# Linear attention with a SwiGLU block: query norms in pieces and another order of copies in the opening of batch 0

## The chip, the cores and the metric

The kernel runs on one core of one Trainium2 chip. The metric is the device time of one execution in microseconds; a median is given where a kernel ran several times. TensorE (PE, with its weight loads PEld), VectorE (DVE), ScalarE (ACT) and GpSimd (POOL) each work through a queue of their own in program order; SyncE (SP) and POOL also issue DMAs.

## The reference

```python
# q, k, v: (8 batches, 8 heads, 576 positions, 64)
q_s = exp(q - max(q, axis=-1));  q_s /= sum(q_s, axis=-1)   # softmax over the 64 features
k_s = exp(k - max(k, axis=2));   k_s /= sum(k_s, axis=2)    # softmax over the positions
kv  = einsum('bhsd,bhse->bhde', k_s, v)                     # 64 x 64 for each head
x   = einsum('bhsd,bhde->bhse', q_s, kv)                    # -> 4608 tokens x 512
g, val = x @ w_gate, x @ w_val                              # 512 -> 1536
out = (g * sigmoid(g) * val) @ w_out                        # 1536 -> 512, float32
```

## The kernel before, in words

Heads are taken in two groups of four (G = 0 and 1). Each of the 128 partitions holds 9 consecutive positions of one head of a pair (T = 9), so a group's q is a tile of 128 x 2 x 576. `BANKS` splits the nine positions into pieces of 5 and 4, as one PSUM bank takes five transposed 128x128 blocks and four the other.

For a group of queries, `exp_of` makes the exponentials on ScalarE, `norm_sum` their sums over 64 features and the reciprocals on VectorE (`rs`, `rr`), and `norm_mul` scales them (`qs`, VectorE). `turn_pe` transposes the scaled queries on TensorE into PSUM (`tp`), and `turn_out` copies them to SBUF (`qt`). For keys, `exp_of` makes `ek`; in batch 0 `key_sum` sums it over positions with small matmuls into `ks`, and its reciprocal `kvr` is made on VectorE. `kv_first` makes K^T V in 36 small matmuls, and `scale_first` scales it by `kvr` into `kn`, half 0 on ScalarE, half 1 on the engine that is given. `x_mm` multiplies `qt` by `kn` into PSUM (`xp`), and `x_out` copies that into `xt`, the transposed input of the feed-forward block: head pair half 0 on ScalarE and half 1 on VectorE.

Everything stands in a `tc.manual_schedule()`: the order in the text is the order of each engine's queue. In the opening SP issues the loads of q and k of both groups; POOL issues v of both groups once k of group 0 has landed, and then the weights in slices of columns (`w_slice`, gate and value in turn, slices of 128, 128, 128, 256, 384, 512), and w_out last. `spin(n)` is n matmuls on zeros that keep TensorE busy; the second call starts with the first sums of group 0. Then comes batch 0 (this is what the diff touches), and behind it `m_unit(0, 576, m)` for the twelve blocks of 128 columns of d_ff: gate matmuls `g_ps` and value matmuls `u_ps`, then silu on ScalarE and the product on VectorE. The first of them takes the four 128-row parts of `xt` by pairs (`by_group`), group 0's pair first.

After it the kernel makes output blocks (`o_mm`), attention of batch b+1 and the feed-forward block of earlier tokens in turn, in chunks of 448 and 512 tokens. PSUM has eight banks, all from one pool (`psp`), so a tile takes the bank that was freed eight tiles before.

Of the kernel before, what the change touches and what calls it, by code (L numbers as in the profile page):

```python
# [8 lines left out]
FP32 = mybir.dt.float32  # L9
BF16 = mybir.dt.bfloat16  # L10
# [5 lines left out]
def kernel(  # L16
# [10 lines left out]
    nc = tc.nc  # L27
# [6 lines left out]
    T = S // 64  # L34
# [3 lines left out]
    BANKS = ((0, 5), (5, T))  # L38
# [3 lines left out]
    at = ctx.enter_context(tc.tile_pool(name="at", bufs=2))  # L42
# [4 lines left out]
    def bank(name):  # L47
        return psp.tile([128, 512], FP32, tag="ps", name=name)
# [57 lines left out]
    def copy(eng, out, in_):  # L106
        if eng is nc.scalar:
            nc.scalar.copy(out=out, in_=in_)
        else:
            eng.tensor_copy(out=out, in_=in_)  # L110
# [3 lines left out]
    st = {}  # L114

    def exp_of(what, b, G, pieces=((0, T),)):
        s = st.setdefault((b, G), {})
        e = s["e" + what] = at.tile([128, T, 2, 64], BF16, tag="e" + what, name="e" + what)
        src = raw[what, b, G].rearrange("p h (t d) -> p t h d", d=64)
        for t0, t1 in pieces:  # L120
            nc.scalar.activation(out=e[:, t0:t1], in_=src[:, t0:t1], func=AF.Exp)  # L121
# [7 lines left out]
    def norm_sum(b, G, pieces=((0, T),)):  # L129
        s = st[b, G]  # L130
        eq2 = s["eq"].rearrange("p t h d -> p (t h) d")
        rs = at.tile([128, 2 * T], FP32, tag="rs", name="rs")
        first = None
        for t0, t1 in pieces:
            i = nc.vector.reduce_sum(  # L135
                out=rs[:, 2 * t0:2 * t1], in_=eq2[:, 2 * t0:2 * t1, :], axis=mybir.AxisListType.X
            )
            first = first or i
        rr = s["rr"] = at.tile([128, 2 * T], FP32, tag="rr", name="rr")
        nc.vector.reciprocal(out=rr, in_=rs)  # L140
        return first

    def norm_mul(b, G, pieces=((0, T),), engs=None):
        s = st[b, G]
        eq2 = s["eq"].rearrange("p t h d -> p (t h) d")
        qs = s["qs"] = at.tile([128, T, 128], BF16, tag="qs", name="qs")
        for (t0, t1), eng in zip(pieces, engs or (nc.vector, nc.vector)):
            n = 2 * (t1 - t0)
            last = eng.tensor_mul(  # L149
                qs[:, t0:t1, :].rearrange("p t (h d) -> p (t h) d", d=64),  # L150
                eq2[:, 2 * t0:2 * t1, :],
                s["rr"][:, 2 * t0:2 * t1].to_broadcast([128, n, 64]),
            )
        return last

    def turn_pe(b, G, i):
        s = st[b, G]
        if i == 0:
            s["qt"] = at.tile([128, T, 128], BF16, tag="qt", name="qt")
        t0, t1 = BANKS[i]  # L160
        tp = s["tp", i] = psp.tile([128, 1024], BF16, tag="ps", name="tp")
        for t in range(t0, t1):
            j = t - t0
            nc.tensor.transpose(  # L164
                out=tp[:, j * 128:(j + 1) * 128], in_=s["qs"][:, t, :], identity=ident
            )

    def turn_out(b, G, i, eng):
        s = st[b, G]
        t0, t1 = BANKS[i]  # L170
        copy(
            eng,
            s["qt"][:, t0:t1, :],
            s["tp", i][:, 0:(t1 - t0) * 128].rearrange("p (t c) -> p t c", c=128),
        )
# [19 lines left out]
    def x_mm(b, G, i):  # L195
        s = st[b, G]
        t0, t1 = BANKS[i]
        xp = [bank("xp") for _ in range(2)]
        for g in range(2):
            for h in range(2):  # L200
                r = slice(64 * h, 64 * h + 64)
                nc.tensor.matmul(
                    out=xp[h][64 * g:64 * g + 64, 0:64 * (t1 - t0)],
                    lhsT=s["kn"][r, g, :],
                    rhs=s["qt"][r, t0:t1, 64 * g:64 * g + 64],
                    start=True, stop=True,
                )
        return xp

    def x_out(b, G, i, xp, engs=(nc.scalar, nc.vector)):  # L210
        t0, t1 = BANKS[i]
        n = 64 * (t1 - t0)
        c0 = b * S + 64 * t0
        for h in (h for h in range(2) if engs[h] is not None):
            copy(engs[h], xt[:, 2 * G + h, c0:c0 + n], xp[h][:, 0:n])
# [137 lines left out]
    with tc.manual_schedule():  # L353
# [16 lines left out]
        for vb in vbs:  # L370
            nc.vector.memset(vb[:, :, :, 64:65], 1.0)

        exp_of("q", 0, 0, BANKS)
        exp_of("k", 0, 0)
        exp_of("q", 0, 1, BANKS)
        first = norm_sum(0, 0, BANKS)
        norm_mul(0, 0, BANKS)
        norm_sum(0, 1, BANKS)

        for c0, n in ((0, 128), (128, 128), (256, 128), (384, 256), (640, 384), (1024, 512)):  # L380
            w_slice(wg, moe_w_gate, c0, n)
# [3 lines left out]
        def spin(n, after=None):  # L385
            idle = bank("idle")
            for _ in range(n):
                i = nc.tensor.matmul(out=idle, lhsT=zero[:, 0:128], rhs=zero, start=True, stop=True)  # L388
                if after is not None:
                    tc.add_manual_dep(i.ins, after.ins.name, SYNC, reason="start of the warm-up")  # L390
                    after = None

        def key_sum(G):
            s = st[0, G]
            ks = bank("ks")
            for t in range(T):
                nc.tensor.matmul(
                    out=ks[:, 0:2], lhsT=s["ek"][:, t, :, :].rearrange("p h d -> p (h d)"), rhs=sel,
                    start=(t == 0), stop=(t == T - 1),
                )  # L400
            s["kvr"] = at.tile([128, 2], FP32, tag="kvr", name="kvr")
            nc.vector.reciprocal(out=s["kvr"], in_=ks[:, 0:2])

        def kv_first(G, t0=0, t1=T):
            s = st[0, G]
            if t0 == 0:
                s["kv"] = [bank("kv") for _ in range(2)]
            for t in range(t0, t1):
                for g in range(2):
                    for h in range(2):  # L410
                        nc.tensor.matmul(
                            out=s["kv"][g][HALF[h], 0:64], lhsT=s["ek"][HALF[g], t, h, :],
                            rhs=v16[G][HALF[g], h, 64 * t:64 * t + 64],
                            start=(t == 0), stop=(t == T - 1),
                        )

        def scale_first(G, eng1):
            s = st[0, G]
            kn = s["kn"] = at.tile([128, 2, 64], BF16, tag="kn1", name="kn1")
            nc.scalar.mul(kn[:, 0, :], s["kv"][0][:, 0:64], s["kvr"][:, 0:1])  # L420
            if eng1 is nc.scalar:
                nc.scalar.mul(kn[:, 1, :], s["kv"][1][:, 0:64], s["kvr"][:, 1:2])
            else:
                nc.vector.tensor_scalar_mul(kn[:, 1, :], s["kv"][1][:, 0:64], s["kvr"][:, 1:2])

        spin(8)
        spin(6, first)
        key_sum(0)
        turn_pe(0, 0, 0)
        turn_pe(0, 0, 1)  # L430
        turn_out(0, 0, 0, nc.scalar)
        exp_of("k", 0, 1)
        turn_out(0, 0, 1, nc.scalar)
        norm_mul(0, 1, BANKS)
        spin(6)
        kv_first(0)
        key_sum(1)
        scale_first(0, nc.scalar)
        turn_pe(0, 1, 0)
        turn_pe(0, 1, 1)  # L440
        turn_out(0, 1, 0, nc.vector)
        turn_out(0, 1, 1, nc.vector)
        xp0 = x_mm(0, 0, 0), x_mm(0, 0, 1)
        kv_first(1, *BANKS[0])
        kv_first(1, *BANKS[1])
        x_out(0, 0, 0, xp0[0], (nc.scalar, None))
        scale_first(1, nc.vector)
        x_out(0, 0, 0, xp0[0], (None, nc.vector))
        x_out(0, 0, 1, xp0[1])
        xp1 = x_mm(0, 1, 0), x_mm(0, 1, 1)  # L450
        x_out(0, 1, 0, xp1[0])
# [18 lines left out]
        exp_of("q", 1, 0)  # L470
        exp_of("q", 1, 1)
        norm_sum(1, 0)
        norm_mul(1, 0)
        norm_sum(1, 1)
        p = [None, None]
# [11 lines left out]
        i = norm_mul(1, 1)  # L487
# [117 lines left out]
```

The softmax here doesn't subtract the row's maximum and nothing guards it: scores larger than these inputs give would overflow.

## Time and profile before

| | us |
|---|---|
| median of 5 runs | 311.88 (311.48 to 312.81) |
| the profiled execution | 311.86 |
| its span, first to last instruction | 310.0 |
| TensorE busy in the span | 301.4 (97%) |
| VectorE busy | 161.6 (52%) |
| ScalarE busy | 146.2 (47%) |
| first gate matmul of the feed-forward block | starts at 14.22 |

Times within the span count from its start. Busy time of TensorE is rough, as matmuls overlap and their ends are modelled; the start-to-start distance of matmuls says more. In the timeline's lines the numbers are start and length, then engine, line and operation, the tile written and the tiles read, shapes, the count, and in brackets the idle time before and who ended it.

### The profile page before, as it was taken

What the parts mean: (1) busy time and instruction counts of PE and PEld (TensorE: products, weight loads), DVE (VectorE), ACT (ScalarE), POOL (GpSimd) and SP (SyncE); (2) the same over time, 40 slices, a digit from 0 to 9 for tenths busy, and PEclk for the clock granted to TensorE, in tenths of its full rate; (3) what the DMA queues carried; (4) which work ended last, traced back from release to release, by engine and by line L of the source; (5) the groups of instructions that cost most, each with busy time, mean ns of one, the idle gap of its engine ahead of it and who ended that gap; (6) DMA issues with size and microseconds to landing.
All of it is one profiled execution on the core that took longest, in us unless ns stands there. A gap on an engine that the chain in (4) does not pass through costs nothing.

```text
span 310.0 us, 5442 instructions
## 1 busy us (share of the span) xinstructions
PE 301.4 (97%) x2157; PEld 149.8 (48%) x2182; DVE 161.6 (52%) x286; ACT 146.2 (47%) x214; POOL 32.1 (10%) x39
## 2 busy tenths in 40 slices
PE   6999999999999999999999999999999999999995
PEld 2578745555444444454444444444444444444443
DVE  3844477945854566365826492639353334433421
ACT  5743469785674375547464737455143113312300
POOL 2960011511100110002000200000000000000000
PEclk9999999999999999999999999999999999999999
DMA  7999999999346815490739352605310302020133
GB/s 275 183 194 207 273 388 389 348 247 378 73 83 196 332 28 118 121 375 33 144 72 354 102 118 61 188 0 107 71 36 0 70 10 58 3 68 8 26 71 103
DMA packets 43018, 45.78 MB, mean 148 GB/s; under 512 B 19568, under 2 KB 28272, under 8 KB 42992
## 3 DMA queue, kind: packets, MB, share of 16 engines
q1 hardware_dynamic: 34096, 39.95, 43.3%
q0 software_dynamic: 8752, 5.31, 12.0%
q8 instruction: 17, 0.28, 0.4%
q10 hardware_dynamic: 144, 0.16, 0.2%
q14 instruction: 9, 0.07, 0.1%
HBM read 37.75 MB, written 9.44 MB: 152 GB/s over the span
## 4 chain that ended last, share of the span: by engine, by line
PE 92%; DMA 4%; POOL 1%; issue 1%; ACT 0%; SPq 0%; DVE 0%
PE u_ps L284 30%; PE g_ps L284 30%; PE o_ps L317 29%; DMA wv<-in_moe_w_val_dram 2%; DMA k<-in_k_dram 2%; PE kv L189 2%; PE xp L245 1%; PE o_ps L338 1%; POOL wg L96 0%; POOL v L361 0%; PE tp L164 0%; POOL v L358 0%; POOL wv L96 0%; ACT xt L259 0%; SPq L77 0%
## 5 line engine op out<-in xcount | busy, mean ns | idle before, releaser
L291 ACT ACTIVATE sg<-g_ps 128x512 bf16<-128x512 f32 (+2 forms) x120 | 64.7, 554 | 133.9 <-PE g_ps L284 120.4
L293 DVE TENSOR_TENSOR hr<-sg,u_ps 128x512 bf16<-128x512 bf16 (+3 forms) x120 | 72.6, 617 | 86.8 <-PE u_ps L284 80.1
L284 PE MATMUL g_ps<-xt,wg 128*128 128x512 bf16 (+2 forms) x473 | 110.9, 358 | 0.5
L284 PE MATMUL u_ps<-xt,wv 128*128 128x512 bf16 (+2 forms) x479 | 111.1, 358 | 0.1
L317 PE MATMUL o_ps<-wo,hr 128*128 128x512 bf16 x403 | 92.5, 379 | 0.9 <-issue 0.2
L284 PEld LDWEIGHTS <-wv 128*128 128x128 bf16 x480 | 46.9, 98 | 46.7 <-DMA wv<-in_moe_w_val_dram 0.4
L284 PEld LDWEIGHTS <-wg 128*128 128x128 bf16 x480 | 46.2, 98 | 45.6 <-issue 0.6
L317 PEld LDWEIGHTS <-hr 128*128 128x128 bf16 x420 | 40.9, 98 | 48.6
L110 DVE COPY o_sb<-o_ps 128x512 f32<-128x512 f32 x33 | 22.4, 680 | 39.0 <-PE o_ps L317 35.4
L124 POOL CAST vb<-v 128x1152 bf16<-128x1152 f32 x14 | 17.1, 1227 | 136.9 <-DMA v<-in_v_dram 134.8
L135 DVE TENSOR_REDUCE rs<-eq 128x18 f32<-128x1152 bf16 (+2 forms) x18 | 21.7, 1214 | 13.1 <-ACT eq L121 13.1
L149 DVE TENSOR_TENSOR qs<-eq,rr 128x1152 bf16<-128x1152 bf16 (+2 forms) x18 | 21.7, 1216 | 0.1
L121 ACT ACTIVATE eq<-q 128x1152 bf16<-128x1152 f32 (+2 forms) x18 | 18.3, 1051 | 5.1 <-DMA q<-in_q_dram 5.0
L121 ACT ACTIVATE ek<-k 128x1152 bf16<-128x1152 f32 (+2 forms) x17 | 17.9, 1101 | 1.0 <-DMA k<-in_k_dram 1.0
L291 ACT ACT_TABLE_LOAD x12 | 15.4, 1283 | 0.2
L121 ACT ACT_TABLE_LOAD x11 | 14.1, 1283 | 0.2
L388 PE MATMUL idle<-zero 128*128 128x512 bf16 x20 | 7.8, 554 | 2.8 <-DVE rs L135 1.6
L259 ACT CAST xt<-xp 128x512 bf16<-128x512 f32 x14 | 7.8, 586 | 4.0 <-PE xp L245 4.0
L260 DVE CAST xt<-xp 128x512 bf16<-128x512 f32 x14 | 9.0, 683 | 0.7 <-PE xp L245 0.7
L189 PEld LDWEIGHTS <-ek 64*64 64x64 bf16 x504 | 6.3, 107 | 1.7 <-ACT ek L121 0.4
L189 PE MATMUL kv<-vb,ek 64*64 64x65 bf16 x504 | 6.7, 194 | 0.0
L245 PE MATMUL xp<-qt,kn 64*64 64x512 bf16 (+1 forms) x112 | 6.7, 292 | 0.0
(44 smaller groups left out, 66.6 us busy)
## 6 DMA issues: line engine op xcount, KB each, us to landing
q<-in_q_dram SPq DMA_DIRECT2D x16, 576.0 KB, 5.1
out_dram<-o_sb SPq DMA_DIRECT2D x70, 128.0 KB, 2.4
k<-in_k_dram SPq DMA_DIRECT2D x12, 576.0 KB, 7.4
v<-in_v_dram SPq DMA_DIRECT2D x12, 576.0 KB, 9.0
wo<-in_moe_w_out_dram POOLq DMA_DIRECT2D x4, 384.0 KB, 15.3
k<-in_k_dram SPq DMA_DIRECT2D x4, 320.0 KB, 8.2
k<-in_k_dram SPq DMA_DIRECT2D x4, 256.0 KB, 8.4
v<-in_v_dram SPq DMA_DIRECT2D x2, 320.0 KB, 7.1
```

The lines of the kernel that those rows point to most:

```text
L110: eng.tensor_copy(out=out, in_=in_)
L121: nc.scalar.activation(out=e[:, t0:t1], in_=src[:, t0:t1], func=AF.Exp)
L124: return nc.gpsimd.tensor_copy(out=vbs[G][:, :, :, 0:64], in_=raw["v", b, G].rearrange("p h (t d) -> p t h d", d=64),)
L135: i = nc.vector.reduce_sum(out=rs[:, 2 * t0:2 * t1], in_=eq2[:, 2 * t0:2 * t1, :], axis=mybir.AxisListType.X)
L149: last = eng.tensor_mul(qs[:, t0:t1, :].rearrange("p t (h d) -> p (t h) d", d=64), eq2[:, 2 * t0:2 * t1, :], s["rr"][:, 2 * t0:2 * t1].to_ ...
L189: nc.tensor.matmul(out=kv[g][HALF[h], c:c + 65], lhsT=ek[HALF[g], t, h, :], rhs=vbs[G][HALF[g], t, h, :], start=(t == 0), stop=(t == T - 1),)
L245: nc.tensor.matmul(out=o[h][HALF[g], c:c + 64 * (t1 - t0)], lhsT=kn[HALF[h], g, G, :], rhs=qt[G][HALF[h], t0:t1, 64 * g:64 * g + 64], star ...
L260: nc.vector.tensor_copy(out=xt[:, 2 * G + 1, c0:c0 + 512], in_=main[G][1])
L284: nc.tensor.matmul(out=gu[a][i][:, 0:w_], lhsT=(wg, wv)[a][:, kk, ms], rhs=xt[:, kk, c:c + w_], start=(kk == 0), stop=(kk == KT - 1),)
L291: nc.scalar.activation(out=sg[:, 0:w_], in_=g_ps[:, 0:w_], func=AF.Silu)
L293: nc.vector.tensor_mul(hr[:, m, r:r + w1], sg[:, 0:w1], u_ps[:, 0:w1])
L317: nc.tensor.matmul(out=o_ps, lhsT=hr[:, m, r0:r0 + 128], rhs=wo[:, m, :], start=(m == 0), stop=(m == MT - 1),)
```

## The change

Four things, all in batch 0's opening. First, `norm_sum` makes a reciprocal for each piece right after its sum, and is called piece by piece, as are `norm_mul` and (for q of group 1) `exp_of`; tiles are made at the first call. Second, the key sums' reciprocal leaves `key_sum` and becomes `key_recip`, placed on its own. Third, the order: the first transposes of group 0 and their copy stand ahead of the key sums and of the second exp piece of group 1; the copy of group 1's first transposes stands on VectorE ahead of the scaling of its second piece; those transposes stand ahead of K^T V of group 0. The copy of x of group 0 is one call for both engines, so that VectorE copies its half before it scales `kn` of group 1. Fourth, the second `spin` has 4 matmuls instead of 6. SP's and POOL's queues keep their order.

```diff
     def norm_sum(b, G, pieces=((0, T),)):
...
         for t0, t1 in pieces:
-            i = nc.vector.reduce_sum(
-                out=rs[:, 2 * t0:2 * t1], in_=eq2[:, 2 * t0:2 * t1, :], axis=mybir.AxisListType.X
-            )
+            r = slice(2 * t0, 2 * t1)
+            i = nc.vector.reduce_sum(out=s["rs"][:, r], in_=eq2[:, r, :], axis=mybir.AxisListType.X)
+            nc.vector.reciprocal(out=s["rr"][:, r], in_=s["rs"][:, r])
             first = first or i
-        rr = s["rr"] = at.tile([128, 2 * T], FP32, tag="rr", name="rr")
-        nc.vector.reciprocal(out=rr, in_=rs)
         return first
...
         exp_of("q", 0, 0, BANKS)
         exp_of("k", 0, 0)
-        exp_of("q", 0, 1, BANKS)
-        first = norm_sum(0, 0, BANKS)
-        norm_mul(0, 0, BANKS)
-        norm_sum(0, 1, BANKS)
+        exp_of("q", 0, 1, BANKS[:1])
+        first = norm_sum(0, 0, BANKS[:1])
+        norm_mul(0, 0, BANKS[:1])
+        norm_sum(0, 0, BANKS[1:])
+        norm_mul(0, 0, BANKS[1:])
...
+            s["ks"] = ks
+
+        def key_recip(G):
+            s = st[0, G]
             s["kvr"] = at.tile([128, 2], FP32, tag="kvr", name="kvr")
-            nc.vector.reciprocal(out=s["kvr"], in_=ks[:, 0:2])
+            nc.vector.reciprocal(out=s["kvr"], in_=s["ks"][:, 0:2])
...
         spin(8)
-        spin(6, first)
+        spin(4, first)
+        turn_pe(0, 0, 0)
+        turn_out(0, 0, 0, nc.scalar)
         key_sum(0)
-        turn_pe(0, 0, 0)
         turn_pe(0, 0, 1)
-        turn_out(0, 0, 0, nc.scalar)
+        exp_of("q", 0, 1, BANKS[1:])
+        norm_sum(0, 1, BANKS[:1])
+        norm_mul(0, 1, BANKS[:1])
+        key_recip(0)
+        turn_out(0, 0, 1, nc.scalar)
         exp_of("k", 0, 1)
-        turn_out(0, 0, 1, nc.scalar)
-        norm_mul(0, 1, BANKS)
+        norm_sum(0, 1, BANKS[1:])
         spin(6)
+        turn_pe(0, 1, 0)
+        turn_out(0, 1, 0, nc.vector)
+        norm_mul(0, 1, BANKS[1:])
         kv_first(0)
         key_sum(1)
+        key_recip(1)
         scale_first(0, nc.scalar)
-        turn_pe(0, 1, 0)
         turn_pe(0, 1, 1)
-        turn_out(0, 1, 0, nc.vector)
         turn_out(0, 1, 1, nc.vector)
         xp0 = x_mm(0, 0, 0), x_mm(0, 0, 1)
         kv_first(1, *BANKS[0])
         kv_first(1, *BANKS[1])
-        x_out(0, 0, 0, xp0[0], (nc.scalar, None))
+        x_out(0, 0, 0, xp0[0])
         scale_first(1, nc.vector)
-        x_out(0, 0, 0, xp0[0], (None, nc.vector))
         x_out(0, 0, 1, xp0[1])
```

More of the change, by code (lines that the diff above doesn't have):

```diff
@@ L117, in exp_of @@
         s = st.setdefault((b, G), {})
-        e = s["e" + what] = at.tile([128, T, 2, 64], BF16, tag="e" + what, name="e" + what)
+        if "e" + what not in s:
+            s["e" + what] = at.tile([128, T, 2, 64], BF16, tag="e" + what, name="e" + what)
+        e = s["e" + what]
         src = raw[what, b, G].rearrange("p h (t d) -> p t h d", d=64)
@@ L131, in norm_sum @@
         eq2 = s["eq"].rearrange("p t h d -> p (t h) d")
-        rs = at.tile([128, 2 * T], FP32, tag="rs", name="rs")
+        if "rs" not in s:
+            s["rs"] = at.tile([128, 2 * T], FP32, tag="rs", name="rs")
+            s["rr"] = at.tile([128, 2 * T], FP32, tag="rr", name="rr")
         first = None
         for t0, t1 in pieces:
-            i = nc.vector.reduce_sum(
-                out=rs[:, 2 * t0:2 * t1], in_=eq2[:, 2 * t0:2 * t1, :], axis=mybir.AxisListType.X
-            )
+            r = slice(2 * t0, 2 * t1)
+            i = nc.vector.reduce_sum(out=s["rs"][:, r], in_=eq2[:, r, :], axis=mybir.AxisListType.X)
+            nc.vector.reciprocal(out=s["rr"][:, r], in_=s["rs"][:, r])
             first = first or i
-        rr = s["rr"] = at.tile([128, 2 * T], FP32, tag="rr", name="rr")
-        nc.vector.reciprocal(out=rr, in_=rs)
         return first
@@ L145, in norm_mul @@
         eq2 = s["eq"].rearrange("p t h d -> p (t h) d")
-        qs = s["qs"] = at.tile([128, T, 128], BF16, tag="qs", name="qs")
+        if "qs" not in s:
+            s["qs"] = at.tile([128, T, 128], BF16, tag="qs", name="qs")
+        qs = s["qs"]
         for (t0, t1), eng in zip(pieces, engs or (nc.vector, nc.vector)):
```

## The prediction

> **What bounds the kernel now.** I read the page first: one core, span 310.0 us, and a chain that is 92% TensorE. Behind the opening, TensorE hardly ever stands still, so a microsecond saved or lost there moves the end by as much, if it gets past the last thing that the opening waits for.
>
> ```profile
> span 310.0 us, 5442 instructions
> PE 301.4 (97%) x2157; PEld 149.8 (48%) x2182; DVE 161.6 (52%) x286; ACT 146.2 (47%) x214; POOL 32.1 (10%) x39
> ...
> PE 92%; DMA 4%; POOL 1%; issue 1%; ACT 0%; SPq 0%; DVE 0%
> ```
>
> So I went to the chain of waits in order of time (start, length, what), cut to the opening:
>
> ```profile
> 6.48 0.86 POOL v L358
> 7.34 1.44 POOL v L361 x2
> 8.78 0.76 POOL wg L96
> 9.54 0.74 POOL wv L96
> 10.28 0.68 POOL wg L96
> 10.96 6.42 DMA wv<-in_moe_w_val_dram
> 17.38 0.05 issue
> 17.43 1.15 PE u_ps L284 x8
> ```
>
> The reader is to see that not one instruction of the attention of batch 0 stands in it. The chain runs over the POOL queue: loads of v, then weight slices, one after the other; the second slice of wv is issued at 10.96 and lands at 17.38, and the up-projection of the second d_ff block (m=1) starts on it at 17.43. The gate matmuls of that block start 0.109 us apart at their end, the last at 17.10, so TensorE could have gone on at 17.21: it waits 0.22 us. That is the slack of the whole opening, and also nearly all that the change can win: with everything before it done earlier, u_ps still starts at about 17.42.
>
> Then I read the timeline of the opening (start, length, engine and line, idle time before it):
>
> ```profile
> 8.37 1.25 ACT L121 ACTIVATE eq<-q 128x640 bf16<-128x640 f32 x2 [1.01 <-DMA q<-in_q_dram]
> 9.14 1.41 DVE L135 TENSOR_REDUCE rs<-eq 128x10 f32<-128x640 bf16 x2 [0.45 <-ACT eq L121]
> ...
> 10.37 1.17 ACT L121 ACTIVATE ek<-k 128x1152 bf16<-128x1152 f32 x1
> ...
> 10.89 1.43 DVE L149 TENSOR_TENSOR qs<-eq,rr 128x640 bf16<-128x640 bf16 x2
> ...
> 12.33 0.90 DVE L110 COPY qt<-tp 128x640 bf16<-128x640 bf16 x2
> 12.37 0.23 PEld L164 LDWEIGHTS <-qs 128*128 128x128 bf16 x4 [0.25 <-DVE qs L149]
> ...
> 12.70 0.44 PE L202 MATMUL xp<-qt,kn 64*64 64x320 bf16 x8
> ...
> 13.52 0.28 DVE L424 TENSOR_SCALAR kn<-kv,kvr 128x64 bf16<-128x64 f32 x1 [0.29 <-PE kv L411]
> ...
> 13.84 0.15 PEld L202 LDWEIGHTS <-kn 64*64 64x64 bf16 x8 [0.53 <-ACT kn L420]
> ...
> 14.22 0.67 PE L284 MATMUL g_ps<-xt,wg 128*128 128x320 bf16 x4
> ```
>
> What sets 14.22: q of group 1 lands (8.35), its exp, then VectorE without a pause to 12.32 (sums, reciprocal, scaling), the last four transposes of group 1 (12.37, TensorE waited for qs), x of group 0, K^T V of group 1, its scaling, x of group 1. The pacemaker is VectorE.
>
> **The change, part by part.** Durations are from the groups by shape: reduce 0.821 and 0.676 us (10 and 8 sums), scaling 0.825 and 0.684, PSUM copy qt 0.492 and 0.424, reciprocal 0.266 (18 wide) and 0.107 (2 wide). An independent follower on VectorE starts some 0.08 us before its forerunner ends (0.821 reduces start 0.737 apart); a dependent one starts 0.034 after it. ScalarE: exp 0.736 and 0.612, starts 0.64 apart; qt copy 0.692 and 0.577.
>
> 1. Norms piece by piece. Reciprocals of 10 and 8 replace each of 18; the trace has none of these. Bounds are 0.107 and 0.266; on the line between the two rows they are 0.187 and 0.167, which I take. Group 0: the scaled first piece is ready at 7.42 instead of 8.09, the second at 8.93 instead of 8.70. The first gain meets TensorE still in its warm-up (four matmuls 0.427 apart from 6.40, so to 8.11 at the cold rate); the loss is hidden, since ScalarE takes the transposed piece only at 10.12.
>
> 2. ScalarE's queue: the copy of the first transposes moves ahead of the second exp piece of q, group 1. Exp piece one 8.37 to 9.11 as before; copy 9.02 to 9.71; exp piece two 9.60 to 10.21 (before: 9.02 to 9.63); copy 10.12 to 10.70; exp of k of group 1 10.60 to 11.76 (before 10.37 to 11.54). Queued behind them are the two scalings of group 0's K^T V. They need K^T V itself, which starts at the landing of v (issued 6.48, 4.7 to land: 11.2 as now); five transposes now stand in front of it and push its end to some 11.86. The scalings start at 11.90, as before. Cost nothing; the cover is the arrival of v and K^T V.
>
> 3. VectorE's queue for group 1, the part that counts. Sum of piece one at 9.14; reciprocal 10.00 (+0.855); scaling 10.22 (+0.22); key reciprocal 10.96 (+0.74); sum of piece two 11.08 (its exp is there at 10.21, so the late exp is hidden by VectorE's own queue); reciprocal 11.79; then the PSUM copy of the first transposes, which are at TensorE from 11.10 to 11.54, at 11.95; and only behind this copy the scaling of piece two, 12.43 to 13.11. Before, this scaling ended at 12.32 and the copy came after it. So the last four transposes start at 13.17 instead of 12.37: 0.80 us later, made up of the copy ahead of it (0.48), two waits between dependent steps (some 0.15) and the split reciprocal (0.1 or so).
>
> 4. x of group 0 stands behind these four transposes in TensorE's queue though it needs none of them: it starts at 13.43 instead of 12.70. Its scaled K^T V is there at 12.43 all the while.
>
> 5. Behind it, as before: K^T V of group 1 (13.70 to 14.16). That it is "right behind x" is not new, the trace has it at 12.97. ScalarE copies x (13.80), then scales kn half 0 (14.20 to 14.52). VectorE: qt copy 13.53, x copy 13.87 (0.481), kn half 1 at 14.27, done 14.56. The x copy now stands ahead of that scaling and costs nothing, for K^T V ends only at 14.16. x of group 1 starts at 14.60 instead of 13.84, the first gate matmul at 14.98 instead of 14.22: +0.76. ScalarE's copies of x end at 15.68, its table load (1.28) 16.96, the first silu at 16.97 instead of 16.23. Eight PSUM banks take two d_ff blocks, so the third block's gate, at about 18.95, is the first that waits for this one; it is long done.
>
> 6. Two warm-up matmuls fewer: nothing if the clock opens as before (their end, 8.97, was followed at once by work that now has its place).
>
> The sum: 0.76 late at the first gate matmul, less 0.22 of slack before the wv slice, is +0.54 us at u_ps of block 1. From there to 38 us TensorE has no pause in the trace (20.57 of 20.57 us), and later weights land at the same times as now, so all of it reaches the end. The profiled execution took 311.86 us (1.86 around its span), as good as the median of the five runs, 311.88: 312.4.
>
> **Rule against row: the clock.** At the start the spins (128x512) are 0.427 apart; the transposes come 0.107 apart up to 9.38 and 0.056 from 9.47; the next spins 0.216. So the rate doubled at about 9.42. The profile's PEclk row reads 9 all along and doesn't show this. The Trainium skill, page "TensorE: Matmul & The Clock Gate", sections Part 1 and Part 4, says that full rate needs a busy stretch of some 3.4 us in windows that run freely, and that transposes do not count as busy in the same way. In the 3.41 us before 9.42 the spins had 2.74 us of busy time, all of TensorE's work 3.02. With four spins instead of six they have some 1.9, and the rest is transposes and two-column key sums. By the row (work of any kind in an unbroken sequence) the rate doubles as before and the sum is 312.4. By the rule it may not double at 9.42 and the second warm-up runs cold; that is the slower rival below. I take the row, as the gapless work is nearly the same, and because the first eight spins (1.22 to 4.81) may open the clock by themselves in other executions.
>
> A second rule: the Trainium skill, page "SBUF — State Buffer", section "SBUF: two separate sides", has VectorE's fast modes keep POOL from writing DMA descriptors, some 3.1 us for 0.6. Between 9.0 and 12.7 VectorE is busy 3.51 of 3.70 us, yet POOL's issues go on 0.73 apart. The reordered VectorE work is of the same kinds: I take zero for it; the rule once on the wv slice would cost 2.5 us.
>
> **Rivals.** (a) Hidden: the reciprocals and waits are shorter than I think or the copy waits less, and the 0.22 us of slack take most of it. For it: the slack is real. Against: the copy ahead of the scaling alone is 0.48. Then 311.7 to 312.1, about 311.9.
> (b) Slower, the clock: the second warm-up (six matmuls from 9.42) goes at 0.427, to 11.98 instead of 10.72. The five transposes at 0.107 end at 12.74, the VectorE copy is 12.78 to 13.27, the scaling behind it ends at 13.94 instead of 13.11: 0.83 more, 313.3. If the clock is still closed when the gate matmuls begin, up to 3.4 us of them run at half rate, 1.7 more: 315.0. It decides from the point where x of group 1 starts after 15.0, since then u_ps of block 1 starts over 0.94 us late.
> (c) VectorE's chain is longer than I sum, by 0.4 or more, another wait on TensorE's side: 312.9 or so.
> (d) Faster: only if the wv slice lands earlier. Neither POOL's queue nor a load is moved; the next slices also land only shortly before their use (the wv slice issued at 13.89 takes 7.3, so 21.2, for u_ps of block 3 at 21.36). A gain of more than 0.2 us has no source: 311.6 at best.
> (e) The change doesn't do what it says: half true, see 5; it is in the sum.
>
> **How the numbers follow.** Main case 0.62, at 312.0 to 312.9, of which 0.05 over 312.8; (a) 0.14; (b) 0.18; (c) 0.03; (d) and the unknown 0.03. A measurement of this kernel tells about 0.3%, 0.94 us, from no change. Slower: 0.05 + 0.18 + 0.03 = 0.26. Same: 0.57 + 0.14 = 0.71. Faster: 0.03. The range 311.7 to 313.5 holds the main case, (a), (c) and the cheap part of (b), and leaves out some 0.17.
>
> **What would show it.** Right: x of group 0 starts near 13.4 behind four transposes that waited for qs; x of group 1 near 14.6, the first gate near 15.0; no wait for the wv slice at u_ps of block 1, which starts near 17.97; that slice still lands near 17.4. (b) shows in second warm-up matmuls 0.427 apart. Wrong: a last transpose before 12.7, or u_ps still waiting for wv; or a slice that lands at another time.

## The result and the profile after

The changed kernel takes 312.78 us (median of 21 runs, 311.62 to 314.82), the kernel before 311.68 (40 runs, 311.21 to 312.94): ratio 1.0036, interval 1.0024 to 1.0049. That is 1.1 us slower where 0.54 was forecast: inside the range, but just over the 0.94 us that the text called the bound of "same", so in the part that it gave 0.26. In the second set of experiments two of the 51 executions of the kernel before took 819 and 1808 us; they are left out.

The profiled execution took 312.64 us, 0.78 more than that of before. Its page, the lines that answer to those of before:

```profile
span 310.8 us, 5440 instructions
PE 301.2 (97%) x2155; PEld 150.2 (48%) x2180; DVE 163.1 (52%) x288; ACT 146.2 (47%) x214; POOL 32.8 (11%) x39
...
PE 90%; DVE 4%; DMA 2%; ACT 1%; issue 1%; SPq 0%
```

TensorE does the same work; the share of VectorE in the chain has gone from 0% to 4%. The chain of waits in order of time says where:

```profile
1.76 6.48 DMA q<-in_q_dram
8.27 0.74 ACT eq L123
9.03 0.83 DVE rs L140
...
11.66 0.20 DVE rr L141
11.87 0.35 DVE qt L110
12.22 0.61 DVE qs L153
12.88 0.41 PE tp L168 x4
13.31 0.34 DVE qt L110
13.65 0.48 DVE xt L110
14.13 0.20 DVE kn L433
14.35 0.47 PE xp L206 x8
14.81 0.60 PE g_ps L288 x4
...
42.29 2.02 DVE qs L153
...
47.33 0.68 PE tp L168 x9
```

Before, the opening's chain ran over POOL and the wv slice; now it runs over q of group 1 and then VectorE step by step, with the copy `qt` (11.87) between the reciprocal and the scaling `qs`, as the prediction had it. x of group 1 starts at 14.35 (13.84 before). And there is a second place that the prediction did not have: in batch 1, at 42.29, one scaling takes 2.02 us. The timeline there:

```profile
41.96 1.14 POOL L126 CAST vb<-v 128x1152 bf16<-128x1152 f32 x1 [20.28 <-DMA v<-in_v_dram]
41.99 0.27 DVE L141 RECIPROCAL rr<-rs 128x18 f32<-128x18 f32 x1
42.29 2.02 DVE L153 TENSOR_TENSOR qs<-eq,rr 128x1152 bf16<-128x1152 bf16 x1
...
47.33 0.45 PE L168 MATMUL tp<-ident,qs 128*128 128x128 bf16 x5 [0.55 <-DVE qs L153]
```

In the profile before, the same scaling starts at 42.11 and takes 1.36, with POOL's cast of v only at 43.02. Here v of batch 1 landed at 41.90 instead of 42.96, the cast was first, and TensorE stood still for 0.55 us. On these two traces alone one would book 0.27 us to the opening (u_ps of block 1 at 17.70 instead of 17.43) and 0.55 to this collision. The experiments say otherwise.

Each timed execution also comes with its mean recorded clock. One stretch of 3.41 us at half clock lowers it by 0.0055. (Values of 0.997 to 0.999 need no such stretch inside the work: in the profile with six matmuls below, at 0.998, the clock is recorded at half only from 308.92 to the end at 310.06.) Eight of the 21 executions of the changed kernel are at 0.995 or less, four of them at 0.981 to 0.982 with 314.3 to 314.8 us. Of the kernel before, 2 of 75 in the first set of experiments are so low, and none of 49 in the second. Where in the span a stretch lies is known only for the profiled executions.

### The profile page after: what moved, and what is told of

The parts are those of the page before. It is cut to its first block, busy times and chain, and to the rows that moved or that the text cites. A ratio compares the mean times of both kernels' runs of the same rounds, so it can differ in the third digit from the quotient of the medians.

```text
span 310.8 us, 5440 instructions
## 1 busy us (share of the span) xinstructions
PE 301.2 (97%) x2155; PEld 150.2 (48%) x2180; DVE 163.1 (52%) x288; ACT 146.2 (47%) x214; POOL 32.8 (11%) x39
## 4 chain that ended last, share of the span: by engine, by line
PE 90%; DVE 4%; DMA 2%; ACT 1%; issue 1%; SPq 0%
PE g_ps L288 30%; PE u_ps L288 30%; PE o_ps L321 26%; DMA q<-in_q_dram 2%; DVE qs L153 2%; PE kv L193 2%; PE xp L249 1%; DVE rs L140 1%; PE o_ps L342 1%; ACT eq L123 1%; ACT L123 0%; PE tp L168 0%; DVE rr L141 0%; SPq L77 0%; DVE qt L110 0%
## 5 line engine op out<-in xcount | busy, mean ns | idle before, releaser
L126 POOL CAST vb<-v 128x1152 bf16<-128x1152 f32 x14 | 17.8, 1271 | 137.4 <-DMA v<-in_v_dram 88.9
L153 DVE TENSOR_TENSOR qs<-eq,rr 128x1152 bf16<-128x1152 bf16 (+2 forms) x18 | 23.1, 1283 | 0.2
```

The lines of the kernel that those rows point to most:

```text
L126: return nc.gpsimd.tensor_copy(out=vbs[G][:, :, :, 0:64], in_=raw["v", b, G].rearrange("p h (t d) -> p t h d", d=64),)
L153: last = eng.tensor_mul(qs[:, t0:t1, :].rearrange("p t (h d) -> p (t h) d", d=64), eq2[:, 2 * t0:2 * t1, :], s["rr"][:, 2 * t0:2 * t1].to_ ...
```

## The experiments

All have five rounds. The kernel before had 311.67 in the first set (75 runs, mean 311.81) and 311.7 in the second (49 runs, mean 311.81), which ran on another chip. The last four experiments are of the second set.

**The copy behind the scaling.**

```diff
-        turn_out(0, 1, 0, nc.vector)
         norm_mul(0, 1, BANKS[1:])
+        turn_out(0, 1, 0, nc.vector)
```

> The changed kernel, with the copy of group 1's first transposes put back behind the scaling of the second piece on VectorE. If the copy ahead of the scaling is what makes the opening late: the last four transposes start some 0.35 us earlier than in the changed kernel (12.88 there, so near 12.5), x of group 1 near 14.0 instead of 14.35, u_ps of block 1 near 17.4, and the time falls by about 0.3 us, to 1.002 to 1.003 of before. If the clock or the collision of batch 1 makes most of the loss: the same shift in the opening, but the time stays within 0.15 us of the changed kernel.

Measured: 312.58, ratio 1.0022 (1.0011 to 1.0033); last transposes at 12.58, x of group 1 at 14.05, u_ps at 17.40. The opening moved by 0.30, as expected (0.05 of it because VectorE began with group 1 that much earlier, 8.98 against 9.03). The median fell by 0.2, which the scatter of 21 and 22 executions does not tell from nothing. The loss doesn't end there: 8 of 22 executions have a clock of 0.995 or less, five of them 0.989 (two stretches) with 312.9 to 313.5.

**Six warm-up matmuls in the changed kernel.**

```diff
-        spin(4, first)
+        spin(6, first)
```

> The changed kernel with six matmuls in the second warm-up instead of four. If the two matmuls fewer keep the clock shut in a part of the executions: the executions of the changed kernel with a recorded clock of 0.98 and 314.3 to 314.8 us (4 of 21) are gone or rare, the median falls by some 0.1 to 0.3 us, to about 312.5. If transposes count as busy like any matmul: no difference, such executions come as often.

Measured: 312.46, ratio 1.0019 (1.0008 to 1.003), mean 312.41 against 312.94. One of 22 executions is at 0.995 or less, none lower.

**The cast made to wait.**

```diff
-        norm_mul(1, 0)
+        i0 = norm_mul(1, 0)
...
-        cast_v(1, 0)
+        c0 = cast_v(1, 0)
+        tc.add_manual_dep(c0.ins, i0.ins.name, SYNC, reason="order of the vector port")
```

> The changed kernel, with POOL's cast of v of batch 1, group 0, made to wait for the scaling of group 0's queries of batch 1 on VectorE. In the profile of the changed kernel the two overlap, the scaling takes 2.02 us instead of 1.36, and TensorE waits 0.55 us for scaled queries at 47.3. If this collision carries the part of the loss that the opening does not: the scaling takes 1.36, the wait at 47.3 is under 0.1, and the time falls by some 0.5 us, to about 312.3. If the collision is chance and rare: the median does not move by more than 0.15 us.

Measured: 312.42, ratio 1.0025 (1.0012 to 1.0039), mean 312.56; 0.36 less than the changed kernel, where 0.5 was expected. The scaling takes 1.36 and the wait of TensorE at 47.3 is gone. With the collision out of the way the times sort by the clock: at 0.999 or more, 311.70 to 312.59 (12 executions, median 311.99); at 0.995, 312.57 to 312.86 (7); at 0.982, 314.30 to 314.62 (3). By medians a stretch with the clock shut costs 0.70 us here, three cost 2.5.

The profiled execution of this kernel is one at 0.995, and shows how it comes about. TensorE's timeline:

```profile
6.28 1.04 PE L393 MATMUL idle<-zero 128*128 128x512 bf16 x4 [1.46 <-DVE rs L140]
7.39 0.45 PE L168 MATMUL tp<-ident,qs 128*128 128x128 bf16 x5
7.68 0.37 PE L402 MATMUL ks<-sel,ek 128*128 128x2 bf16 x9
8.95 0.61 PE L168 MATMUL tp<-ident,qs 128*128 128x128 bf16 x4 [0.90 <-DVE qs L153]
9.35 2.72 PE L393 MATMUL idle<-zero 128*128 128x512 bf16 x6
```

and its stretches (length, TensorE busy and matmuls, granted clock, DMA share, GB/s):

```profile
5.00:8.50 3.50, 1.69 (x18) 1.00 1.03 373
8.50:12.00 3.50, 3.05 (x12) 0.51 1.23 170
```

The first eight warm-up matmuls have opened the clock, recorded from 5.07 on. So the four of the second warm-up fly by in 1.04 us, TensorE then waits 0.90 for VectorE, and after one stretch that is half idle the clock is shut from 8.485 to 11.898, just over the six matmuls that follow: they are 0.427 apart and take 2.72. x of group 1 starts at 15.01. The same stretches with six matmuls, from the run above, whose clock also opened early (5.14):

```profile
5.00:8.50 3.50, 1.95 (x20) 1.00 1.03 360
8.50:12.00 3.50, 2.84 (x60) 1.00 1.23 181
```

In both runs 5.00 to 8.50 is almost exactly one stretch of the clock's record (5.07 to 8.49 and 5.14 to 8.55, with the same busy time). Here 1.95 us busy kept the clock and 1.69 did not.

**Four warm-up matmuls in the kernel before.**

```diff
-        spin(6, first)
+        spin(4, first)
```

> The kernel before with four matmuls in the second warm-up instead of six, nothing else. If the number of warm-up matmuls alone shuts the clock in some executions: some of them (one in ten to one in four) take 1.5 to 2.5 us longer with a recorded clock near 0.98; the median moves up by 0 to 0.2 us. If the clock does not mind: ratio 1.000 and no such execution.

Measured: 311.89, ratio 1.0011 (0.9998 to 1.0023), mean 312.12. Nine of 22 executions are at 0.992 to 0.995; none is near 0.98, where some had been expected. So two matmuls fewer are enough to shut the clock in four executions of ten. What a shut stretch costs here is not shown: these nine have a median of 311.89, the other thirteen 311.86 (the eight at 1.000 have 311.50, but the five at 0.997 to 0.999 have 312.19 to 313.34). The interval of the ratio holds 1, and one execution at 1.000 and 314.49, unexplained, makes 0.11 of the 0.31 by which the mean rose. The profiled one again opened early, at 5.51. Its rows, cut at the clock's own record, and below them the one row for the run that comes next (the kernel before with six matmuls and a waiting cast, open from 4.44):

```profile
5.51:8.93 3.42, 2.02 (x21) 1.00 1.02 343
8.93:12.34 3.41, 3.41 (x46) 0.50 1.22 160
...
4.44:7.85 3.41, 1.86 (x16) 1.00 1.03 388
```

So the sum of busy time does not decide: a stretch with 2.02 us shut the clock, one with 1.86 kept it. The warm-up matmuls alone do sort the stretches: 1.04 us of them in the two that shut it, 1.47 to 1.72 in the four early ones that kept it.

Over all kernels with four matmuls (changed, and three of these runs) 35 of 87 executions are at 0.995 or less; with six, where the clock was noted, 4 of 210. The profiles agree: six of the ten opened early (4.44 to 5.51), and of these the two with four matmuls shut again and the four with six did not. None of the four that opened late (9.43 to 10.18) shut again.

**The kernel before with the cast made to wait**, by the same edit as above.

> The kernel before, with POOL's cast of v of batch 1, group 0, made to wait for the scaling of group 0's queries of batch 1. If the kernel before meets the collision too, only less often: its executions at 312.2 to 312.9 with an open clock (5 of 42) mostly go, the median falls by 0.05 to 0.1 us and the mean by 0.1 to 0.2 (ratio 0.9995). If those executions come from something else: no difference.

Measured: 311.47, ratio 0.9987 (0.9979 to 0.9995), mean 311.49 against 311.81. Only one of 22 is still over 312. So the kernel before loses 0.32 us in the mean to the collision, nearly as much as the changed kernel does (312.94 against 312.56). With six matmuls in both, the changed kernel loses about as much: 0.28 (312.41 less the 312.13 of the next run). So it adds little to the difference, though each of these three numbers is good to 0.2 to 0.5 only. This version is 0.13% faster than the kernel before.

**The order alone**: the changed kernel with six matmuls and with the waiting cast.

> The changed kernel with six warm-up matmuls and with the cast made to wait: of the change, only the order and the pieces are left. If clock and collision carry the rest: u_ps of block 1 starts 0.2 to 0.3 us later than in the kernel before and the time is 311.85 to 312.0, the executions with a recorded clock of 0.995 or less are 1 in 20 or fewer. If the order is the main cost: 312.3 or more.

Measured: 312.05, ratio 1.0009 (0.9996 to 1.0022), mean 312.13, 1 of 14 executions below 0.995. The right yardstick is the run above, which has the same cast: 312.05 less 311.47 is 0.58 us for order and pieces (0.3 to 0.7 in 95 of 100 cases, when the executions of both runs are drawn again at random). That lies between the two cases of the expectation. The copy ahead of the scaling on VectorE:

```profile
11.74 0.20 DVE L141 RECIPROCAL rr<-rs 128x8 f32<-128x8 f32 x1
11.87 0.44 DVE L110 COPY qt<-tp 128x640 bf16<-128x640 bf16 x1
12.22 0.68 DVE L153 TENSOR_TENSOR qs<-eq,rr 128x512 bf16<-128x512 bf16 x1
```

It costs 0.35 from start to start, where 0.48 had been put down.

**The order, with the copy behind the scaling.**

```diff
-        turn_out(0, 1, 0, nc.vector)
         norm_mul(0, 1, BANKS[1:])
+        turn_out(0, 1, 0, nc.vector)
```

> As the run on the order alone, but the copy of group 1's first transposes behind the scaling of the second piece. If this copy is the cost that is left: u_ps of block 1 near 17.4, time 311.6 to 311.7, as the kernel before. If the cost is spread over the split reciprocals and the order of copies of x: half of the shift stays, 311.75 to 311.9.

Measured: 311.75, ratio 1.0000 (0.999 to 1.0011): 0.30 less than the order alone, so about half of the 0.58 is this one copy; with 14 executions each, the scatter just fails to rule out nothing. The other 0.28 over the kernel before with the waiting cast is left for the pieces and the other moves together; these were not taken apart.

**The order, with x of group 0 ahead of the last transposes.**

```diff
-        turn_pe(0, 1, 1)
-        turn_out(0, 1, 1, nc.vector)
         xp0 = x_mm(0, 0, 0), x_mm(0, 0, 1)
+        turn_pe(0, 1, 1)
+        turn_out(0, 1, 1, nc.vector)
```

> As the run on the order alone, but x of group 0 ahead of the last four transposes of group 1 on TensorE. If VectorE's queue sets the time of x of group 1 by itself: x of group 0 starts near 12.6 instead of 13.1, x of group 1 moves by less than 0.1, and the time is that of the run on the order alone within 0.1 us. If the place of x of group 0 in TensorE's queue is what costs: x of group 1 starts 0.3 us or more earlier and the time falls to 311.6.

Measured: 312.07, ratio 1.001 (1.000 to 1.002), the time of the order alone. TensorE's timeline:

```profile
12.30 0.64 PE L206 MATMUL xp<-qt,kn 64*64 64x320 bf16 x8
12.88 0.40 PE L168 MATMUL tp<-ident,qs 128*128 128x128 bf16 x4
...
14.10 0.72 PE L206 MATMUL xp<-qt,kn 64*64 64x320 bf16 x8 [0.42 <-ACT kn L429]
14.75 0.66 PE L288 MATMUL g_ps<-xt,wg 128*128 128x320 bf16 x4
...
17.93 0.80 PE L288 MATMUL u_ps<-xt,wv 128*128 128x320 bf16 x5
```

x of group 0 starts 1.0 us before that of the order alone (12.30 against 13.29), x of group 1 starts 0.33 earlier (14.10 against 14.43), but takes 0.72 instead of 0.47, and the first gate matmul is at 14.75 against 14.83. (In this one profile the wv slice landed at 17.88, so that u_ps of block 1 waited for it.) The expectation that x of group 1 hardly moves was wrong, its verdict on the time right. The second half of x of group 1 needs VectorE's half of `kn`, and that starts at 14.05 here and at 14.13 in the order alone. So VectorE's queue holds it, and the place of x of group 0 in TensorE's queue is not what costs.

## Why the prediction was right or wrong

1. The mechanism of the main case holds, in kind and in size: 0.58 us for the order against 0.54. But two of its terms were off and cancel, so that the size is in part luck. The shift at x of group 1 is 0.50 in the two profiles, not 0.76: the copy costs 0.35 instead of 0.48, and q of group 1 landed 0.11 earlier in the profile after (8.24 against 8.35). Counted from that landing the shift is about 0.6. The sum also let x of group 0 start 0.26 after the four transposes; both profiles have 0.33. And the slack of 0.22 before the wv slice is mostly not there.

2. That slack was the step that failed, and with it the claim that nothing can be won. In the profile before, the wv slice landed at 17.38. In nine other profiles it landed at 15.6 to 16.8 in eight, and at 17.88 in one. The first kernel's own profile was the exception: usually TensorE gets to u_ps of block 1 last, and a later opening counts in full. An earlier one should count as well: in the profile of the kernel before with the waiting cast, where the exp of q of group 1 starts at 7.88 instead of 8.37, u_ps starts at 16.68. But no run made the opening shorter on purpose, so a gain is not shown.

3. "Two warm-up matmuls fewer: nothing" was the second failed step. It was argued with the first eight matmuls: if they open the clock by themselves, the second warm-up does not matter. The reverse is so. With the clock open, the four matmuls take half as long, the stretch becomes half idle, and the clock shuts again when it is next needed. By means, the four matmuls cost 0.53 us in the changed kernel (312.94 less 312.41), 0.43 with the waiting cast (312.56 less 312.13), and 0.31 in the kernel before. When the executions are drawn again at random, the first is 0.1 to 1.0, the other two 0 to 0.9 and 0 to 0.7: that more executions have a shut clock is plain, its mean price is not well known. This term, put at nothing, makes the larger part of what the forecast lacked (1.1 less 0.54). The rival (b) had the price nearly right (0.83 for one stretch, measured 0.70; 2.5 for several, measured 2.5), its place, and the point from which it decides (x of group 1 at 15.0; 15.01 in the execution shown, at 312.62), but took the wrong group of executions, those that open late, for the exposed ones. The profile after is one that opened late: the clock was recorded open from 10.18, 0.74 later than before (9.43), and the first two of its next six warm-up matmuls were still 0.427 apart. It cost nothing there, as the transposes behind them were done at 11.52, before VectorE's copy at 11.87. That several stretches also cost 2.5 is in part luck: the price was worked out for a clock still shut at the gate matmuls, and no trace shows where the several stretches lay. It also gave a single time for what is a mixture: 8 of 21 executions.

4. Not foreseen: the collision of cast and scaling in batch 1. In the two profiles it looks like two thirds of the loss, but the kernel before loses about as much to it (0.32); in the profile taken of it the cast came late.

The sum by means: order 0.6, clock 0.4 to 0.5, collision the same as before within 0.06 (0.38 or 0.28, less 0.32), together 1.0 to 1.2 us, where 1.13 was measured (312.94 less 311.81). Each term is uncertain by 0.3 to 0.5, so the sum agrees without fixing the shares. The medians give less for the clock, as it strikes four executions in ten.

5. Right: ScalarE's moves cost nothing by themselves (both scalings of group 0's K^T V start at 11.98 and 12.19, against 11.90 and 12.11), POOL's issues stay 0.73 apart, and no slice of weights lands later for the change. The split reciprocals took 0.218 and 0.204 us; 0.187 and 0.167 had been read off the line between two rows.

Open: whether transposes count for the clock. At shutting it looks as if they did not (the stretch with 2.02 us, 1.04 of them warm-up). At opening it looks as if something beside warm-up matmuls did: 1.89 us of these in 3.03 of work opened the clock in the profile of the copy behind the scaling (6.09 to 9.51), while 2.21 us of them alone did not in the profile before (2.61 to 6.02). The shut stretches held fewer warm-up matmuls and also idle time; no run here changed one without the other. Why the clock stays shut for three stretches in some executions of the changed kernel and never in the kernel before with four matmuls was not traced either: no profile fell on such an execution.

## What to carry to other kernels

A slack read from one trace is that execution's slack: before a gain is written off as hidden behind a transfer, look at how far its landing moves between executions. Filler matmuls are worth the time that they hold TensorE busy at the rate of the moment: four of them filled 1.9 us in the profile after and 1.04 where the clock had opened early. If it can open early, count them at the fast rate. And a difference between two traces that hangs on which of two engines comes first by a few tenths of a microsecond should be tested in both kernels before it is charged to the change.

## What the runs showed of the hardware that was not expected

The clock does not need an idle stretch to shut: it shut after stretches of 3.41 us with 1.69 and 2.02 us of work. With 1.86 to 1.96 it stayed open, so the amount of work alone does not tell. Its records come in stretches of 3.413 us, at a phase that differs from execution to execution (open from 4.44 to 10.18 in the profiles).

POOL's cast (128x1152, float32 to bf16) and VectorE's scaling (the same size, bf16) exclude each other: whoever is second waits. The scaling took 2.02 and 2.23 us instead of 1.36 where the cast was first, the cast 2.03 and 2.37 instead of 1.14 where the scaling was. One case of the second kind, from the run with the copy behind the scaling (for the first kind see the profile after):

```profile
42.16 1.36 DVE L153 TENSOR_TENSOR qs<-eq,rr 128x1152 bf16<-128x1152 bf16 x1
42.49 2.03 POOL L126 CAST vb<-v 128x1152 bf16<-128x1152 f32 x1 [20.64 <-DMA v<-in_v_dram]
```

VectorE's sums next to it took 1.34 to 1.35 as ever. This is what the Trainium skill, page "SBUF — State Buffer", section "SBUF: two separate sides", describes as an exclusive lock of a shared port; it held here for two instructions, while the DMA issues on POOL showed nothing of it. In batch 1 the two start within 0.33 us of each other in four of the five profiles without the added dependency (0.91 apart in the profile before), so small shifts decide the order. One dependency that fixes it makes the kernel before 0.13% faster.
